# One written order of small steps for all five engines, and a first chunk in two halves of 256 tokens

## The chip, the cores and the metric

The kernel runs on one core of a Trainium2 chip. The metric is device microseconds of one execution; the kernel before takes 420.45 us (median of 3 runs, 420.3 to 420.76).

The engines are called by the names of the profile: PE (TensorE, its weight loads apart as PEld), DVE (VectorE), ACT (ScalarE), POOL (GpSimd) and SP (SyncE). POOL issues the loads from memory, SP the transposes by DMA and the stores of the output.

## What is computed

An attention of the linear kind over 8 batches of 8 heads, 576 tokens each, 64 wide, and behind it a two-layer block with an ELU over all 4608 tokens:

```python
def phi(x):
    proj = np.einsum('bhsd,df->bhsf', x, w_phi)                # 64 -> 128
    proj = proj - np.max(np.abs(proj), axis=-1, keepdims=True)
    return np.concatenate([np.exp(proj), np.exp(-proj)], axis=-1)
q_p, k_p = phi(q), phi(k)
kv = np.einsum('bhsf,bhsd->bhfd', k_p, v);  z = np.sum(k_p, axis=2)
num = np.einsum('bhsf,bhfd->bhsd', q_p, kv)
den = np.einsum('bhsf,bhf->bhs', q_p, z)[..., None] + 1e-06
x = (num / den) as 4608 x 512                                  # heads side by side
h = x @ w_in                                                   # 512 -> 2048
out = np.where(h > 0, h, np.exp(np.minimum(h, 0)) - 1) @ w_out # 2048 -> 512
```

## The kernel before

The attention goes by 16 groups n of four heads (two groups a batch). One group passes these stages; the name of a stage's product in PSUM is the one that the profile shows:

- `transpose_in`: k and q come with tokens on the partitions and are transposed to kT and qT. For the first four groups PE does it (tile `tr`) and DVE copies it out; for the others it is a DMA transpose on SP.
- `stage_k`, three pieces: PE projects (pk), DVE takes the largest absolute value of each row (mk), ACT writes both exponentials (EK). `scale_v`: ACT takes the exponentials of the row maxima (em), POOL multiplies v by them (vs, four large ones a group).
- `stage_qmax`, three pieces: PE projects q with tokens on the partitions (pm), DVE takes the row maxima (mq), splits them into a high and a low bf16 part (mhl), and they are transposed (mT).
- `stage_q`, three pieces: PE projects q with features on the partitions and subtracts the maxima by a product with the selector `sel` (pq); ACT writes both exponentials (Eq).
- `stage_kv`: 72 small products (kv), copied out by DVE (kv_sb).
- `stage_pn`, two pieces: 20 products (pn), of which DVE divides (den, rec, xp). `transpose_x` brings xp into xT_sb, for the first two groups by PE (trx) and DVE, then by two DMA transposes a piece.

The ELU block goes by 9 chunks of 512 tokens. Each has 16 first steps `moe_mm1` (four matmuls ph of 512 columns; ACT takes the exponential e_sb, POOL its minimum with 1, DVE the maximum with ph, into gT) and 16 second steps `moe_mm2` (four matmuls po; after every fourth step ACT copies o_sb and SP stores it). Chunk 0 needs only the tokens of batch 0, chunk c up to 7 those of batch c, and chunk 8 comes last.

The order is written as a list of pieces of one group, between which a number of `moe` steps is emitted from a list `pending`; a chunk joins that list some pieces after its batch is done (`LAG`). From this order and its own estimates a scheduler sets the order on each engine when the program is built. In PSUM the first 38 pieces use four tiles of two banks; after them there are two tiles of two banks (for pk, pm, pq, kv and pn) and four of one bank (for ph, po and the transposes).

The core's 16 DMA engines move the loads in the order in which POOL issues them. A load on POOL waits in the program until the load eight places before it has landed, since it takes over that one's semaphore.

Of the kernel before, what the change touches and what calls it, by code (L numbers as in the profile page):

```python
# [12 lines left out]
ALU = mybir.AluOpType  # L13
ACT = mybir.ActivationFunctionType


@with_exitstack
def kernel(
# [34 lines left out]
    PE_TRANSPOSED_X = 2  # L53
# [10 lines left out]
    pools = {}  # L64

    def two_banks(shape, dtype, name):
        return pools["pj"].tile(shape, dtype, name=name, tag="pj")

    def one_bank(shape, dtype, name):
        if "mp" in pools:  # L70
            return pools["mp"].tile(shape, dtype, name=name, tag="mp")
        return pools["pj"].tile(
            [shape[0], 2 * shape[1]] + shape[2:], dtype, name=name, tag="pj"
        )[:, 0:shape[1]]

    natural = {}

    def load(name, src, b, p0=0, p1=H // 2):
        if (name, b) not in natural:
            natural[name, b] = io.tile([P, H // 2, NS, D], BF16, name=name + "n")  # L80
        nc.gpsimd.dma_start(  # L81
            out=natural[name, b][:, p0:p1].rearrange("p r s d -> p r (s d)"),
            in_=src[b]
            .rearrange("h s d -> (h s d)")
            .rearrange("(pr q x) -> q pr x", q=P, x=NS * D)[:, p0:p1],
        )


    w_f32 = consts.tile([P, F], FP32)
    for par in range(2):  # L90
        nc.sync.dma_start(out=w_f32[par * D:(par + 1) * D, :], in_=w_phi)
    load("k", k, 0, 0, 2)
    ident = consts.tile([P, P], BF16)
    make_identity(nc, ident)
    load("k", k, 0, 2, 4)
    load("q", q, 0, 0, 2)
    load("v", v, 0, 0, 2)
    load("q", q, 0, 2, 4)
    load("v", v, 0, 2, 4)

    w_bd = consts.tile([P, 2, F], BF16)
    nc.vector.memset(w_bd, 0.0)
    for par in range(2):
        r = slice(par * D, (par + 1) * D)
        nc.vector.tensor_copy(w_bd[r, par, :], w_f32[r, :])

    sel_small = consts.tile([P, NI], BF16)
    nc.vector.memset(sel_small, 0.0)  # L110
    for off in (0, NI, D, D + NI):
        nc.gpsimd.affine_select(
            out=sel_small, in_=sel_small, pattern=[[-1, NI]],
            compare_op=ALU.not_equal, fill=-1.0, base=-off, channel_multiplier=1,
        )
    sel = consts.tile([P, NI, F], BF16)
    nc.vector.tensor_copy(sel, sel_small.unsqueeze(2).to_broadcast((P, NI, F)))

    load("k", k, 1)
    load("q", q, 1)  # L120
    w_in_sb = consts.tile([P, N_CT, DFF], BF16)
    w_in_r = moe_w_in.rearrange("(ct p) j -> p ct j", p=P)
    for c0 in range(0, N_CT, 2):
        nc.gpsimd.dma_start(out=w_in_sb[:, c0:c0 + 2, :], in_=w_in_r[:, c0:c0 + 2, :])
    load("v", v, 1)
    w_out_sb = consts.tile([P, N_JT, DM], BF16)
    w_out_r = moe_w_out.rearrange("(jt p) o -> p jt o", p=P)
    for jt in range(0, N_JT, 8):
        nc.gpsimd.dma_start(
            out=w_out_sb[:, jt:jt + 8, :], in_=w_out_r[:, jt:jt + 8, :]  # L130
        )

    mhl_bufs = []
    for j in range(2):
        mhl_j = consts.tile([P, 2, D], BF16, name=f"mhl{j}")
        nc.vector.memset(mhl_j, 0.0)
        mhl_bufs.append(mhl_j)

# [11 lines left out]
    def out_rows(tile_index):  # L150
        bp, t = divmod(tile_index, 9)
        rows = []
        for half in range(2):
            if t == 4:
                b, s = 2 * bp + half, 8
            else:
                b, t4 = (2 * bp, t) if t < 4 else (2 * bp + 1, t - 5)
                s = 4 * (t4 % 2) + t4 // 2 + 2 * half
# [5 lines left out]
    moe_state = {}  # L164

    def moe_mm1(ch, jt):
        t0 = ch * CHUNK
        if jt == 0:
            moe_state[ch] = moep.tile([P, N_JT, CHUNK], BF16, name="gT")
        gT = moe_state[ch]  # L170
        ph = one_bank([P, CHUNK], FP32, "ph")
        for ct in range(N_CT):
            nc.tensor.matmul(  # L173
                ph,
                w_in_sb[:, ct, jt * P:(jt + 1) * P],
                xT_sb[:, ct, t0:t0 + CHUNK],
                start=(ct == 0),
                stop=(ct == N_CT - 1),
            )
        e_sb = epool.tile([P, CHUNK], FP32, name="e_sb")  # L180
        nc.scalar.activation(e_sb, ph, ACT.Exp)  # L181
        nc.gpsimd.tensor_scalar(  # L182
            e_sb, e_sb, 1.0, 0.0, op0=ALU.min, op1=ALU.max
        )
        nc.vector.scalar_tensor_tensor(  # L185
            gT[:, jt, :], e_sb, -1.0, ph, op0=ALU.add, op1=ALU.max
        )

    def moe_mm2(ch, tt, part):
        gT = moe_state[ch]  # L190
        if part == 0:
            moe_state[ch, tt] = one_bank([P, DM], FP32, "po")
        po = moe_state[ch, tt]
        for jt in range(4 * part, 4 * part + 4):
            nc.tensor.matmul(  # L195
                po,
                gT[:, jt, tt * P:(tt + 1) * P],
                w_out_sb[:, jt, :],
                start=(jt == 0),
                stop=(jt == N_JT - 1),  # L200
            )
        if part == 3:
            o_sb = opool.tile([P, DM], FP32, name="o_sb")
            nc.scalar.copy(o_sb, po)  # L204
            for half, rows in enumerate(out_rows(ch * (CHUNK // P) + tt)):
                nc.sync.dma_start(out=rows, in_=o_sb[half * D:(half + 1) * D])

    pending = []

    def enqueue_chunk(ch):  # L210
        for jt in range(N_JT):
            pending.append((moe_mm1, ch, jt))
        for tt in range(CHUNK // P):
            for part in range(4):
                pending.append((moe_mm2, ch, tt, part))

    def emit_moe():
        if pending:
            fn, *args = pending.pop(0)
            fn(*args)  # L220

    st = {}
# [3 lines left out]
    SLOTS = (  # L226
        ((0, 0), (0, 2), (1, 0), (1, 2), (0, 3)),
        ((1, 4), (1, 6), (0, 5), (0, 7), (1, 7)),
    )

    def pe_transpose(dst, blocks):

        for j0 in range(0, len(blocks), 5):
            part = blocks[j0:j0 + 5]
            tr = one_bank([P, 8, P], BF16, "tr")
            for j, blk in enumerate(part):
                nc.tensor.transpose(tr[:, j, :], blk, ident)
            nc.vector.tensor_copy(dst[:, j0:j0 + len(part), :], tr[:, 0:len(part), :])

    def transpose_in(n, name):  # L240
        if n >= NG:
            return
        b, g = divmod(n, 2)
        nat = natural[name, b][:, 2 * g:2 * g + 2].rearrange("p r s d -> p (r s d)")
        dst = tpool.tile([P, NI, P], BF16, name=name + "T")
        if n < PE_TRANSPOSED:
            pe_transpose(dst, [nat[:, i * P:(i + 1) * P] for i in range(NI)])
        else:
            nc.sync.dma_start_transpose(out=dst, in_=nat)
        st[name + "T", n] = dst  # L250

    def row_max(m, pj, c):
        nc.vector.tensor_reduce(  # L253
            m[:, 6 * c:6 * c + 6], pj, axis=AX.X, op=ALU.max,
            apply_absolute_value=True,
        )

    def project_k(n, c):
        kT = st["kT", n]
        pj = two_banks([P, 8, F], FP32, "pk")  # L260
        for i3 in range(3):
            nc.tensor.matmul(  # L262
                pj[:, 2 * i3:2 * i3 + 2, :].rearrange("p r f -> p (r f)"),
                kT[:, 3 * c + i3, :],
# [4 lines left out]
        return pj[:, 0:6, :]  # L269

    def stage_k(n, c):
        if c == 0:
            st["EK", n] = work.tile([P, 2, 2 * NS, F], BF16, name="EK")
            st["mk", n] = small.tile([P, 2 * NS], FP32, name="mk")
            st["em", n] = small.tile([P, 2, 2 * NS], FP32, name="em")
            st["vs", n] = work.tile([P, 2, 2 * NS, D + 1], BF16, name="vs")
        EK, mk = st["EK", n], st["mk", n]
        pj = project_k(n, c)
        row_max(mk, pj, c)
        for sg in range(2):  # L280
            nc.scalar.activation(  # L281
                EK[:, sg, 6 * c:6 * c + 6, :], pj, ACT.Exp, scale=1.0 - 2.0 * sg
            )
        if c > 0:
            scale_v(n, c - 1)

    def scale_v(n, pr):
        b, g = divmod(n, 2)
        mk, em, vs = st["mk", n], st["em", n], st["vs", n]
        r = slice(pr * NS, (pr + 1) * NS)  # L290
        for sg in range(2):
            nc.scalar.activation(  # L292
                em[:, sg, r], mk[:, r], ACT.Exp, scale=2.0 * sg - 1.0
            )
        for sg in range(2):
            nc.gpsimd.tensor_tensor(  # L296
                vs[:, sg, r, 0:D],
                natural["v", b][:, 2 * g + pr],
                em[:, sg, r].unsqueeze(2).to_broadcast((P, NS, D)),
                op=ALU.mult,  # L300
            )
        nc.gpsimd.tensor_copy(vs[:, :, r, D], em[:, :, r])

    def stage_qmax(n, c):
# [18 lines left out]
        if c < 2:  # L323
            return
# [258 lines left out]
```

## Time and profile before

| | |
|---|---|
| runs | 420.45 us median (420.3 to 420.76) |
| profiled execution | 421.46 us, its span 419.7 us |
| busy | PE 370.2, DVE 247.8, ACT 246.8, POOL 189.7 us |
| mean clock granted to PE | 0.958 |
| first ph matmul | 43.29 us |
| moved by DMA | 40.08 MB, mean 95 GB/s |

The span runs from the first to the last instruction of the profiled execution. In lines of the profile a group of instructions has its source line, its engine and operation, what it writes and reads, how often it stands, its busy time and mean duration, and after the second bar the time that the engine stood idle before it and what ended most of that. Rows of the timeline begin with the start and the length in us, and end, in brackets, with the idle time before them and its cause.

### The profile page before, as it was taken

To read this page: it belongs to the slowest core of one execution; us is meant where nothing else is said; L and a number is where in the kernel's file an instruction comes from. 1 tells how busy PE (TensorE), PEld (TensorE's weight loads), DVE (VectorE), ACT (ScalarE), POOL (GpSimd) and SP (SyncE) were. 2 spreads that over 40 slices of the span, in tenths; PEclk is the share of its full clock that TensorE was granted. 3 is DMA by queue.
4 is the path that set the end of the run, shared out by engine and by line. 5 is a ranking of instruction groups with operands and counts; after the bars stand their busy time and mean duration, and the time that the engine had idled before them with its cause. 6 is when DMAs were issued, how large, how long until landed. Compare 5 with 4: busy or idle time off the path is not lost.

```text
span 419.7 us, 9524 instructions
## 1 busy us (share of the span) xinstructions
PE 370.2 (88%) x3856; PEld 194.0 (46%) x3856; DVE 247.8 (59%) x419; ACT 246.8 (59%) x437; POOL 189.7 (45%) x281
## 2 busy tenths in 40 slices
PE   3567787995989998999899989999799989999995
PEld 2356335452545454454445544545354535444442
DVE  4978566752776467645866477647754943360630
ACT  2747435753676667756774777487647772551631
POOL 8840651615265346534663366236604570450620
PEclk9659888998899999999999999999999999999999
DMA  8999972399128952879179813652143002203113
GB/s 120 210 211 208 194 105 44 64 169 183 33 58 131 157 104 45 112 117 176 30 114 146 161 27 58 135 110 36 30 89 74 19 16 66 66 2 75 25 27 75
DMA packets 69564, 40.08 MB, mean 95 GB/s; under 512 B 49936, under 2 KB 64400, under 8 KB 69520
## 3 DMA queue, kind: packets, MB, share of 16 engines
q0 software_dynamic: 15344, 18.35, 28.1%
q1 hardware_dynamic: 54176, 21.12, 27.3%
q8 instruction: 30, 0.49, 0.5%
q14 instruction: 14, 0.11, 0.1%
HBM read 36.77 MB, written 9.44 MB: 110 GB/s over the span
## 4 chain that ended last, share of the span: by engine, by line
PE 34%; DVE 22%; issue 18%; ACT 11%; POOL 10%; DMA 4%; POOLq 0%; ACTq 0%
PE po L195 17%; PE ph L173 10%; DVE gT L185 8%; POOL vs L296 5%; DVE mk L253 4%; POOL e_sb L182 4%; ACT EK L281 3%; DMA qT<-qn 3%; ACT Eq L370 3%; DVE xp L422 3%; ACT e_sb L181 3%; DVE mq L319 2%; PE pn L410 2%; PE kv L388 2%; PE pk L262 1%
## 5 line engine op out<-in xcount | busy, mean ns | idle before, releaser
L173 PE MATMUL ph<-xT_sb,w_in_sb 128*128 128x512 bf16 x576 | 143.0, 389 | 15.5 <-DVE gT L185 10.0
L185 DVE SCALAR_TENSOR_TENSOR gT<-e_sb,ph 128x512 bf16<-128x512 f32 x144 | 94.3, 684 | 75.7 <-POOL e_sb L182 75.5
L195 PE MATMUL po<-w_out_sb,gT 128*128 128x512 bf16 x576 | 137.6, 380 | 0.5 <-DVE gT L185 0.5
L182 POOL TENSOR_SCALAR e_sb<-e_sb 128x512 f32<-128x512 f32 x144 | 86.7, 613 | 110.9 <-ACT e_sb L181 110.7
L181 ACT ACTIVATE e_sb<-ph 128x512 f32<-128x512 f32 x144 | 83.4, 606 | 61.8 <-PE ph L173 61.6
L296 POOL TENSOR_TENSOR vs<-vn,em 128x576 bf16<-128x576 bf16 x64 | 72.4, 1152 | 59.4 <-ACT em L292 43.7
L173 PEld LDWEIGHTS <-w_in_sb 128*128 128x128 bf16 x576 | 54.4, 99 | 76.2 <-issue 16.5
L281 ACT ACTIVATE EK<-pk 128x768 bf16<-128x768 f32 x96 | 72.6, 814 | 23.4 <-DVE mk L253 21.5
L370 ACT ACTIVATE Eq<-pq 128x768 bf16<-128x768 f32 x96 | 73.5, 824 | 16.0 <-PE pq L360 15.7
L195 PEld LDWEIGHTS <-gT 128*128 128x128 bf16 x576 | 52.4, 98 | 55.6 <-DVE gT L185 1.0
L319 DVE TENSOR_REDUCE mq<-pm 128x6 f32<-128x768 f32 x48 | 45.9, 957 | 36.6 <-PE pm L312 36.5
L204 ACT COPY o_sb<-po 128x512 f32<-128x512 f32 x36 | 21.1, 587 | 67.0 <-PE po L195 42.9
L253 DVE TENSOR_REDUCE mk<-pk 128x6 f32<-128x768 f32 x48 | 45.5, 952 | 11.8 <-PE pk L262 11.8
L410 PEld LDWEIGHTS <-Eq 128*128 128x128 bf16 x640 | 24.0, 97 | 8.0 <-DVE kv_sb L396 0.6
L262 PE MATMUL pk<-w_bd,kT 128*128 128x256 bf16 x144 | 25.6, 293 | 1.9 <-ACT EK L281 0.8
L422 DVE TENSOR_TENSOR xp<-pn,rec 128x640 bf16<-128x640 f32 x32 | 26.4, 824 | 1.2 <-DVE rec L420 0.3
L410 PE MATMUL pn<-kv_sb,Eq 128*128 128x65 bf16 x640 | 25.4, 194 | 0.5 <-DVE kv_sb L396 0.4
L388 PEld LDWEIGHTS <-EK 64*128 64x128 bf16 x1152 | 20.9, 99 | 7.1 <-ACT Eq L370 3.5
L388 PE MATMUL kv<-vs,EK 64*128 64x65 bf16 x1152 | 22.9, 197 | 1.2 <-ACT Eq L370 1.1
L81 POOL DMA_DIRECT2D qn<-in_q_dram x9 | 6.8, 760 | 33.2 <-PE po L195 13.3
L312 PE MATMUL pm<-w_bd,qT 64*128 64x128 bf16 x288 | 18.2, 230 | 4.0 <-ACT EK L281 1.5
L262 PEld LDWEIGHTS <-kT 128*128 128x128 bf16 x144 | 14.1, 103 | 14.8 <-issue 5.2
(42 smaller groups left out, 164.8 us busy)
## 6 DMA issues: line engine op xcount, KB each, us to landing
out_dram<-o_sb SPq DMA_DIRECT2D x72, 128.0 KB, 2.5
kn<-in_k_dram POOLq DMA_DIRECT2D x7, 576.0 KB, 7.3
qn<-in_q_dram POOLq DMA_DIRECT2D x7, 576.0 KB, 7.7
vn<-in_v_dram POOLq DMA_DIRECT2D x7, 576.0 KB, 10.1
w_in_sb<-in_moe_w_in_dram POOLq DMA_DIRECT2D x2, 1024.0 KB, 19.0
w_out_sb<-in_moe_w_out_dram POOLq DMA_DIRECT2D x2, 1024.0 KB, 28.0
xT_sb<-xp SPq DMA_TRANSPOSE x56, 2.4
kn<-in_k_dram POOLq DMA_DIRECT2D x2, 288.0 KB, 5.5
```

What stands on the lines that cost most here:

```text
L173: nc.tensor.matmul(ph, w_in_sb[:, ct, jt * P:(jt + 1) * P], xT_sb[:, ct, t0:t0 + CHUNK], start=(ct == 0), stop=(ct == N_CT - 1),)
L181: nc.scalar.activation(e_sb, ph, ACT.Exp)
L182: nc.gpsimd.tensor_scalar(e_sb, e_sb, 1.0, 0.0, op0=ALU.min, op1=ALU.max)
L185: nc.vector.scalar_tensor_tensor(gT[:, jt, :], e_sb, -1.0, ph, op0=ALU.add, op1=ALU.max)
L195: nc.tensor.matmul(po, gT[:, jt, tt * P:(tt + 1) * P], w_out_sb[:, jt, :], start=(jt == 0), stop=(jt == N_JT - 1),)
L253: nc.vector.tensor_reduce(m[:, 6 * c:6 * c + 6], pj, axis=AX.X, op=ALU.max, apply_absolute_value=True,)
L281: nc.scalar.activation(EK[:, sg, 6 * c:6 * c + 6, :], pj, ACT.Exp, scale=1.0 - 2.0 * sg)
L296: nc.gpsimd.tensor_tensor(vs[:, sg, r, 0:D], natural["v", b][:, 2 * g + pr], em[:, sg, r].unsqueeze(2).to_broadcast((P, NS, D)), op=ALU.mult,)
L319: nc.vector.tensor_reduce(mq[:, 6 * c:6 * c + 6].rearrange("p (i r) -> p r i", r=2), pj[:, :, 0:3, :], axis=AX.X, op=ALU.max, apply_absolu ...
L370: nc.scalar.activation(Eq[:, sg, :, :, 3 * c * D:3 * (c + 1) * D].rearrange("p h r x -> p r h x"), pj[:, :, 0:3 * P].rearrange("p r (h x) ...
L388: nc.tensor.matmul(kv[:, hi, pr, sg, :], EK[rows, sg, pr * NS + s, :], vs[rows, sg, pr * NS + s, :], start=(s == 0), stop=(s == NS - 1),)
L410: nc.tensor.matmul(pn[:, hi, t, :], Eq[:, sg, hi, par, i0 * D:(i0 + 2) * D], kv_sb[:, hi, pr, sg, :], start=(sg == 0), stop=(sg == 1),)
```

## The change

The stages are cut into steps of one engine each (43 kinds, such as `k_mm`, `k_exp`, `k_max`), a string names 1709 steps by one letter each, and the program is written in exactly that order: `manual_schedule` leaves the order on each engine as written. The order was worked out elsewhere by list scheduling. A part of it:

```diff
+ORDER = """
+eabecedjfkfAjgBhkBAhCeBjfABkjiBCliBlkAmDgmlCBFlemBAmDfCBFBMNECEMNDAOEPBQMENBFCSEDUETTFEMVOENPWQM
...
+    pjp = ctx.enter_context(tc.tile_pool(name="pjp", bufs=2, space=bass.MemoryType.PSUM))
+    mpp = ctx.enter_context(tc.tile_pool(name="mpp", bufs=4, space=bass.MemoryType.PSUM))
+
+    ctx.enter_context(tc.manual_schedule(engines=None))
...
+    FIRST = 2
+    PIECES = (((0, 4), (4, 7), (7, 9)), ((0, 3), (3, 6), (6, 9)))
...
+    def m_split(n, part):
+        if n < FIRST:
+            p = ((0, 4), (4, NI))[part]
+        else:
+            p = (0, NI)
+        hi = mhl[n % 2][:, :, p[0]:p[1]]
+        mq = st["mq", n][:, :, p[0]:p[1]]
+        eng = nc.gpsimd if n < PE_TRANSPOSED else nc.vector
+        eng.tensor_copy(hi, mq)
+        eng.tensor_tensor(
+            mhl[n % 2][:, :, NI + p[0]:NI + p[1]], mq, hi, op=ALU.subtract
+        )
...
+    def x_parts(n, part):
+        if n < FIRST:
+            return [(pr, t) for pr in range(2) for t in ((0, 1), (2, 3, 4))[part]]
+        return [(part, t) for t in range(5)]
...
+    chunk_parts = [
+        (ch, jt, h, h + w)
+        for ch in range(N_CHUNK)
+        for w in [CHUNK // 2 if ch == 0 else CHUNK]
+        for h in range(0, CHUNK, w)
+        for jt in range(N_JT)
+    ]
...
+        M=(m_mm, groups(*THIRDS, first=HALVES)), N=(m_max, groups(*THIRDS, first=HALVES)),
+        O=(m_split, m_parts),
...
+        p=(h_mm, chunk_parts), q=(h_exp, chunk_parts), r=(h_min, chunk_parts),
+        s=(h_elu, chunk_parts),
+        t=(o_mm, [(*x, part) for x in o_tiles for part in range(4)]),
+        u=(o_copy, o_tiles), v=(o_store, o_tiles),
     )
...
+    queues = {letter: (fn, iter(args)) for letter, (fn, args) in STEPS.items()}
+    for letter in "".join(ORDER.split()):
+        fn, args = queues[letter]
+        fn(*next(args))
```

For groups 0 and 1 the tokens are placed so that the first 256 of chunk 0 need only the first piece of four (of nine) of pm and pq and the first part of pn: chunk 0 is computed in two halves, with 32 first steps of 256 columns instead of 16 of 512, and its second half needs the other pieces. For those groups q is cut 4, 3, 2 instead of 3, 3, 3, mhl is split in two parts, and xT gets each part for two heads' columns at once. For the first four groups mhl is written by POOL instead of DVE. The two large and four small PSUM tiles now serve from the start. The loads come in smaller parts for k of batch 0, v of batch 0 in one, and w_in ahead of k and q of batch 1.

On POOL, in the head of the program, this is how the last loads and the first products stand before (vn and w_out_sb are loads like w_in_sb; vs is v times em):

```order
L124 DMA w_in_sb<-in_moe_w_in_dram 128x2x2048
L112 AFFINE_SELECT sel_small<-sel_small 128x9
L124 DMA w_in_sb<-in_moe_w_in_dram 128x2x2048
L81 DMA vn<-in_v_dram 128x4x576
L129 DMA w_out_sb<-in_moe_w_out_dram 128x8x512 x2
L296 TENSOR_TENSOR vs<-vn,em 128x9x64 x2
L302 CAST vs<-em 128x2x9
```

(the loads of k and q of batch 1 stand just ahead of these, and those of batch 2 follow after all vs of groups 0 and 1), and this is how they stand now:

```order
L194 DMA w_in_sb<-in_moe_w_in_dram 128x2x2048 x2
L185 DMA kn<-in_k_dram 128x4x576
L185 DMA qn<-in_q_dram 128x4x576
L198 DMA w_out_sb<-in_moe_w_out_dram 128x8x512 x2
L185 DMA vn<-in_v_dram 128x4x576
L275 CAST vs<-em 128x2x9
L185 DMA kn<-in_k_dram 128x4x576
L185 DMA qn<-in_q_dram 128x4x576
L275 CAST vs<-em 128x2x9
L266 TENSOR_TENSOR vs<-vn,em 128x9x64 x2
L310 CAST mhl_96<-mq 128x2x4
L311 TENSOR_TENSOR mhl_96<-mq,mhl_96 128x2x4
```

What moved: w_in stands ahead of the loads of batch 1, the loads of k and q of batch 2 stand ahead of the first vs, and group 0's mhl stands behind two vs. The second qn load here takes over the semaphore of w_in's first half.

On DVE, where the maxima of group 0 are made ready and what follows from them, before (mq and mk are row maxima of q and k, mT the transposed maxima, kv_sb a copy):

```order
L319 TENSOR_REDUCE mq<-pm 128x2x3
L238 COPY qT<-tr 128x640
L327 CAST mhl_131<-mq 128x2x9
L238 COPY qT<-tr 128x512
L328 TENSOR_TENSOR mhl_131<-mq,mhl_131 128x2x9
L238 COPY mT<-tr 128x128
L319 TENSOR_REDUCE mq<-pm 128x2x3 x3
L327 CAST mhl_133<-mq 128x2x9
L328 TENSOR_TENSOR mhl_133<-mq,mhl_133 128x2x9
L396 CAST kv_sb<-kv 128x520
```

and now:

```order
L297 TENSOR_REDUCE mq<-pm 128x2x4
L322 COPY mT<-tr 128x128
L297 TENSOR_REDUCE mq<-pm 128x2x3
L248 TENSOR_REDUCE mk<-pk 128x6
L409 CAST kv_sb<-kv 128x520
L297 TENSOR_REDUCE mq<-pm 128x2x2
L322 COPY mT<-tr 128x128
L443 TENSOR_SCALAR den<-pn 128x2x4
L444 RECIPROCAL rec<-den 128x2x4
L446 TENSOR_TENSOR xp<-pn,rec 128x2x4x64
```

The mhl rows are gone from DVE, the first mT is copied after four of nine pieces of each group's q, and the first xp, of 8 instead of 10 parts, comes before the rest of the maxima.

More of the change, by code (lines that the diff above doesn't have):

```diff
@@ L76 @@
[L76 to L91, printed above, removed]
@@ L92 @@
-    load("k", k, 0, 0, 2)
-    ident = consts.tile([P, P], BF16)
[L94 to L99, printed above, removed]
+        return mpp.tile(shape, dtype, name=name, tag="mp")
+    ident = consts.tile([P, P], BF16)
     w_bd = consts.tile([P, 2, F], BF16)
[L102 to L105, printed above, removed]
@@ L122 @@
     w_in_r = moe_w_in.rearrange("(ct p) j -> p ct j", p=P)
-    for c0 in range(0, N_CT, 2):
-        nc.gpsimd.dma_start(out=w_in_sb[:, c0:c0 + 2, :], in_=w_in_r[:, c0:c0 + 2, :])
-    load("v", v, 1)
     w_out_sb = consts.tile([P, N_JT, DM], BF16)
     w_out_r = moe_w_out.rearrange("(jt p) o -> p jt o", p=P)
[L128 to L137, printed above, removed]
+    mhl = [consts.tile([P, 2, D], BF16, name=f"mhl{j}") for j in range(2)]
@@ L189, in moe_mm2 @@
[L189 to L206, printed above, removed]
@@ L240, in transpose_in @@
[L240 to L255, printed above, removed]
-        )
@@ new lines, in start, with weights @@
+    def start():
+        w_f32 = epool.tile([P, CHUNK], FP32, name="e_sb")[:, 0:F]
+        for par in range(2):
+            nc.sync.dma_start(out=w_f32[par * D:(par + 1) * D, :], in_=w_phi)
+        st["w_f32"] = w_f32
+        make_identity(nc, ident)
+    def weights():
+        nc.vector.memset(w_bd, 0.0)
+        nc.vector.memset(sel_small, 0.0)
+        for j in range(2):
+            nc.vector.memset(mhl[j], 0.0)
+        for par in range(2):
+            r = slice(par * D, (par + 1) * D)
+            nc.vector.tensor_copy(w_bd[r, par, :], st["w_f32"][r, :])
@@ L357, in stage_q, with places @@
-        for i3 in range(3):
+            r = []
+            for j in range(w):
+                i = PLACE_OF[own][par][p0 + j]
+                if r and i == PLACE_OF[own][par][p0 + j - 1] + 1:
+                    r[-1][2] += 1
+                else:
+                    r.append([j, i, 1])
+            runs.append(r)
+        def places(par, j, m):
+            return pj[:, par, 0:w * P].rearrange("p (h i t) -> p h i t", h=2, i=w)[
+                :, :, j:j + m, :
+            ]
+        for x in range(max(len(r) for r in runs)):
+            for par in range(2):
+                if x >= len(runs[par]):
+                    continue
+                j, i, m = runs[par][x]
+                rows = slice(par * D, (par + 1) * D)
+                nc.tensor.matmul(
+                    places(par, j, m),
+                    w_bd[rows, par, :],
+                    qT[rows, i:i + m, :].rearrange("p i (h t) -> p h i t", h=2),
+                    start=(x == 0),
+                    stop=False,
+                )
@@ L358, in stage_q @@
+        for j in range(w):
             for par in range(2):
@@ L550, with h_mm @@
-    after_piece()
-    while pending:
-        emit_moe()
+                out=xT_sb[:, ct, mixed_col(b):mixed_col(b) + D].unsqueeze(1),
+                in_=xp[D:P, 4].rearrange("p h d -> p (h d)"),
+            )
+    def h_mm(ch, jt, h0, h1):
+        ph = one_bank([P, CHUNK], FP32, "ph")[:, h0:h1]
+        for ct in range(N_CT):
+            nc.tensor.matmul(
+                ph,
+                w_in_sb[:, ct, jt * P:(jt + 1) * P],
+                xT_sb[:, ct, ch * CHUNK + h0:ch * CHUNK + h1],
+                start=(ct == 0),
+                stop=(ct == N_CT - 1),
+            )
+        st["ph", ch, jt, h0] = ph
@@ new lines, in o_mm, with o_copy @@
+    def o_mm(ch, tt, part):
+        po = get(("po", ch, tt), lambda: one_bank([P, DM], FP32, "po"))
+        for jt in range(4 * part, 4 * part + 4):
+            nc.tensor.matmul(
+                po,
+                st["gT", ch][:, jt, tt * P:(tt + 1) * P],
+                w_out_sb[:, jt, :],
+                start=(jt == 0),
+                stop=(jt == N_JT - 1),
+            )
+    def o_copy(ch, tt):
+        st["o", ch, tt] = opool.tile([P, DM], FP32, name="o_sb")
+        nc.scalar.copy(st["o", ch, tt], st["po", ch, tt])
@@ new lines, in o_store, with groups @@
+    def o_store(ch, tt):
+        for half, rows in enumerate(out_rows(ch * (CHUNK // P) + tt)):
+            nc.sync.dma_start(out=rows, in_=st["o", ch, tt][half * D:(half + 1) * D])
+    def groups(*tails, first=None):
+        if first is None:
+            return [(n, *x) for n in range(NG) for x in tails]
+        head = [(n, *x) for part in first for n in range(FIRST) for x in part]
+        return head + [(n, *x) for n in range(FIRST, NG) for x in tails]
+    PAIR = [(0,), (1,)]
+    THIRDS = [(c,) for c in range(3)]
@@ new lines, with blocks @@
+    THIRDS2 = [(c, sg) for c in range(3) for sg in range(2)]
+    HALVES = ([(0,)], [(1,), (2,)])
+    HALVES2 = (THIRDS2[:2], THIRDS2[2:])
+    EACH = ([(0,)], [(1,)])
+    PT = PE_TRANSPOSED
+    def blocks(name, n):
+        cut = 3 if (name, n) == ("k", 0) else 5
+        return [(name, n, 0, cut), (name, n, cut, NI)]
+    m_parts = groups((0,), first=EACH)
+    chunk_parts = [
[4 more added lines that the diff above has]
+        for jt in range(N_JT)
+    ]
@@ L556 @@
+    queues = {letter: (fn, iter(args)) for letter, (fn, args) in STEPS.items()}
+    for letter in "".join(ORDER.split()):
+        fn, args = queues[letter]
+        fn(*next(args))
+    assert all(next(args, None) is None for _, args in queues.values())
 _INS = ['q', 'k', 'v', 'w_phi', 'moe_w_in', 'moe_w_out']
```

504 lines of the change are left out of this document (240 added, 264 removed).

## The prediction

> **What bounds the kernel now.** I read the page first, then the busy time by stretches, then TensorE's (PE's) instructions in order of time.
>
> ```profile
> span 419.7 us, 9524 instructions
> PE 370.2 (88%) x3856; PEld 194.0 (46%) x3856; DVE 247.8 (59%) x419; ACT 246.8 (59%) x437; POOL 189.7 (45%) x281
> GB/s 120 210 211 208 194 105 44 64 169 183 33 58 131 157 104 45 112 117 176 30 114 146 161 27 58 135 110 36 30 89 74 19 16 66 66 2 75 25 27 75
> ```
> PE is the fullest engine, and 49.5 us of its span are idle. The next fence cuts the span where the first matmul of chunk 0 (43.29), the first of chunk 1 that had all its tokens (103.88) and the attention-free end (359.83) stand; 119.5 to 334.6 is five whole batches.
>
> ```profile
> 0.00:43.29 43.29, 24.21 (x414) 17.77 (x415) 31.67 (x61) 22.77 (x39) 24.50 (x40) 0.80 1.09 188
> 43.29:103.88 60.59, 49.80 (x511) 25.62 (x507) 34.78 (x59) 32.51 (x58) 26.60 (x38) 0.89 0.82 122
> 103.88:359.83 255.95, 240.95 (x2681) 125.71 (x2682) 159.30 (x267) 167.17 (x299) 119.00 (x172) 0.99 0.49 86
> 119.50:334.60 215.10, 201.92 (x2272) 105.87 (x2271) 137.96 (x231) 144.91 (x261) 104.65 (x151) 1.00 0.55 93
> 359.83:419.70 59.87, 55.25 (x256) 24.85 (x254) 22.00 (x32) 24.37 (x41) 19.59 (x32) 0.99 0.19 45
> ```
> The columns after the length are PE, PEld, DVE, ACT, POOL, clock, DMA share, GB/s. The last stretch is full but for its 4.6 us drain; the first three are not.
>
> Busy time flatters PE, since matmuls overlap in it. So I price PE's work by the distance between starts:
>
> ```profile
> 206.72 1.03 PE L173 MATMUL ph<-xT_sb,w_in_sb 128*128 128x512 bf16 x4
> 209.32 1.02 PE L173 MATMUL ph<-xT_sb,w_in_sb 128*128 128x512 bf16 x4 [1.57 <-DVE gT L185]
> ...
> 218.57 1.32 PE L388 MATMUL kv<-vs,EK 64*128 64x65 bf16 x72
> 219.82 0.82 PE L195 MATMUL po<-w_out_sb,gT 128*128 128x512 bf16 x3
> ...
> 221.90 0.79 PE L410 MATMUL pn<-kv_sb,Eq 128*128 128x65 bf16 x20
> 222.53 1.89 PE L195 MATMUL po<-w_out_sb,gT 128*128 128x512 bf16 x8
> 224.26 0.49 PE L262 MATMUL pk<-w_bd,kT 128*128 128x256 bf16 x3
> 224.58 1.89 PE L195 MATMUL po<-w_out_sb,gT 128*128 128x512 bf16 x8
> ...
> 235.84 0.34 PE L350 MATMUL pq<-qT,w_bd 64*128 64x384 bf16 x2
> 236.01 0.33 PE L360 MATMUL pq<-mT,sel 64*128 64x128 bf16 x6
> 236.18 0.33 PE L312 MATMUL pm<-w_bd,qT 64*128 64x128 bf16 x6
> 236.44 1.47 PE L173 MATMUL ph<-xT_sb,w_in_sb 128*128 128x512 bf16 x6
> ...
> 373.48 13.98 PE L195 MATMUL po<-w_out_sb,gT 128*128 128x512 bf16 x64
> 387.29 13.98 PE L173 MATMUL ph<-xT_sb,w_in_sb 128*128 128x512 bf16 x64
> ```
> 64 wide matmuls take 387.29 - 373.48 = 13.81 us, a step of four 0.863, a chunk 27.6. A head group takes kv 1.25, two pn 1.26, three pk 0.96, three times pq 0.34 and pm 0.26: 5.3 us. One chunk and two groups are 38.2 us, and a batch takes 215.1/5 = 43.0: PE loses 4.8 us a batch. 1.7 of it is the gap at 207.6, where the next four ph wait for a PSUM bank that VectorE's gT frees; the rest are pauses of 0.1 to 0.5.
>
> **The change, term by term.** Nothing on PE gets cheaper, so what can be won is PE's lost time, and I sum four stretches.
>
> *To the first ph.* The new order puts the loads of w_in ahead of k and q of batch 1, moves two more loads (k and q of batch 2) ahead of group 0's vs on POOL, moves the mhl pair of the first four groups from DVE to POOL behind those vs, and gives the head two large PSUM tiles where it had four. The rows:
>
> ```profile
> kn<-in_k_dram POOLq DMA_DIRECT2D x7, 576.0 KB, 7.3
> DMA to landing us min/median/max: 17.1/19.0/20.9
> 8.20 0.74 POOL L124 DMA_DIRECT2D w_in_sb<-in_moe_w_in_dram  x1
> 10.70 0.76 POOL L81 DMA_DIRECT2D vn<-in_v_dram  x1 [0.75 <-DMA qn<-in_q_dram]
> 19.86 3.92 DVE L327 CAST mhl<-mq 128x18 bf16<-128x18 f32 x1
> 106.56 1.51 ACT L370 ACTIVATE Eq<-pq 128x768 bf16<-128x768 f32 x2 [1.38 <-PE pq L360]
> ...
> L181 ACT ACTIVATE e_sb<-ph 128x512 f32<-128x512 f32 x144 | 83.4, 606 | 61.8 <-PE ph L173 61.6
> L370 ACT ACTIVATE Eq<-pq 128x768 bf16<-128x768 f32 x96 | 73.5, 824 | 16.0 <-PE pq L360 15.7
> L296 POOL TENSOR_TENSOR vs<-vn,em 128x576 bf16<-128x576 bf16 x64 | 72.4, 1152 | 59.4 <-ACT em L292 43.7
> L319 DVE TENSOR_REDUCE mq<-pm 128x6 f32<-128x768 f32 x48 | 45.9, 957 | 36.6 <-PE pm L312 36.5
> L422 DVE TENSOR_TENSOR xp<-pn,rec 128x640 bf16<-128x640 f32 x32 | 26.4, 824 | 1.2 <-DVE rec L420 0.3
> L396 DVE CAST kv_sb<-kv 128x520 bf16<-128x520 f32 x16 | 11.1, 695 | 4.2 <-PE kv L388 4.2
> L302 POOL CAST vs<-em 128x18 bf16<-128x18 f32 x32 | 8.3, 259 | 0.0
> L238 DVE COPY kT<-tr 128x640 bf16<-128x640 bf16 x4 | 1.9, 485 | 1.9 <-PE tr L237 1.9
> ```
> The row at 10.70 shows the wait: POOL stood until an older load (qn) had landed. The new q load of batch 2 waits in the same way for the load eight places back, which is now w_in's first half. That half landed at 8.20 + 17.1 = 25.3 us; without k and q of batch 1 ahead of it (2 x 0.59 MB at 211 GB/s, 5.6 us) it lands at 19.7. Behind the wait stand all vs of groups 0 and 1. POOL then does the load (0.78), a cast (0.26), two vs (2.3) and the mhl pair, which it never did: at least DVE's 0.2, at most the 3.92 that the cast took on DVE; nearest is POOL's cast of the same 18 elements, 2 x 0.26. That gives 23.5.
> From there, with only two large tiles, each product waits for the tile before last: copy 0.2, mq 0.9, mk 0.9 and latencies (25.8); pq 0.9 at the low clock, two Eq a third wider 2.2 (28.9); kv copy 0.7, mq 0.6 (30.2); pn 0.8, xp chain 1.1 (32.1); copy 0.2, mq 0.9, xT copy 0.4, mq 0.6 (34.2); kv 1.3, copy 0.7 (36.2); pn 0.8, xp 1.1 (38.1); three copies 1.1, xT copy 0.4 (39.6). First ph at **40 us**, against 43.29. Ends: 34, where POOL isn't held and vs start as now; 46, where w_in lands no earlier than now.
> Rule against row: the Trainium skill's "SBUF — State Buffer" (section "SBUF: two separate sides") says that VectorE and GpSimd share a port pair as an exclusive lock, and who loses blocks. The 3.92 us row lies beside vs and agrees. By that rule alone the move to POOL would bring 3.7 us and the first ph would come at 36; I don't take it, since the pair now queues behind those vs.
>
> *Chunk 0, to the first ph of chunk 1.* PE: 16 ph steps and 16 po steps, 27.6 us, and by the order 2.8 groups, 14.8: 42.4. A 256-wide matmul costs half (pk's three take 0.32, 0.107 each), so the halves cost PE nothing, and their loads hide as pk's do. ACT: 33 wide exponentials (two in 1.51, so 0.76 each) 25, four copies and six small pairs 4, 32 half-wide ones between 0.30 and 0.61, taken 0.40: 12.8, in all 42. So ACT is as full as PE, and 16 more instructions on it lie on the path (3 us, in the sum). With both full I take 1.2 times the work: **51 us**; ends 42.4 and 60.6 (as now). Chunk 1 starts at 91, against 103.88.
>
> *To the end of the attention.* 256 us now, in a dense order 256 x 38.2/43.0 = 227. Chunk steps and attention steps alternate more finely now, with po between the ph, which attacks the 1.7 us gap; the 0.1 us pauses at each change to a 64-row product stay. I halve the loss: **241 us**; ends 227 and 256. Where a gT no longer holds the ph, ACT is late next (145 of 215 us busy).
>
> *End.* The same 256 matmuls and drain: **59.9 us** (here each wait has its cover: nothing but ELU work is left).
>
> 40 + 51 + 241 + 59.9 = 391.9 us of span. The profiled execution took 421.46 us for its span of 419.7; the median, 420.45, lies 0.75 above that span, so 392.7. Any change under 0.2% (0.8 us) couldn't be told from none.
>
> **Rivals.**
> *The middle stays as it is* (other pauses replace the gT gap: ACT is busy 145/5 = 29 us of each batch, mostly where a chunk's ph run, and feeds both kinds of step): 91 + 256 + 59.9 + 0.75 = 408.
> *Dense*: POOL isn't held and PE waits little: 36 + 46 + 233 + 59.9 + 0.75 = 376. Against it: in chunk 0 ACT is as full as PE.
> *Slower: late transposes.* One place now shows the price:
>
> ```profile
> 98.26 0.60 PE L173 MATMUL ph<-xT_sb,w_in_sb 128*128 128x512 bf16 x2
> 103.88 1.89 PE L173 MATMUL ph<-xT_sb,w_in_sb 128*128 128x512 bf16 x4 [5.01 <-DMA xT_sb<-xp]
> ```
> The ph waited 5.0 us for xT and then ran four matmuls in 1.89 instead of 1.03. In the new order only two or three po steps (1.7 to 2.6 us) and a small product or two lie between the last xT transpose of a batch and the first ph of its chunk, at chunks 1, 2, 4, 5, 6 and 7, and PE can't pass a waiting ph. 5.0 + 0.9 at all six is 35 us: 428. It decides from 4.6 us each. Against it: only there did loads fill the DMA engines; over the five batches their share is 0.55.
> By the Trainium skill, "TensorE: Matmul & The Clock Gate" (section "Part 1: The HAM clock gate"), an idle window of some 3.4 us halves PE's clock for a next one; the slow four agree, and by that rule each such wait would cost about 6.7 us, six of them 433.
> *No change*: every term at its upper end, 46 + 60.6 + 256 + 59.9 = 422.
>
> **How the numbers follow.** Forecast (384 to 401) 0.52, middle unchanged 0.21, dense 0.15, slower 0.09, no change 0.03. Leaving out what lies under 376 and over 409 leaves about 2 in 10 outside. Faster 0.52 + 0.21 + 0.15 = 0.88, same 0.03, slower 0.09.
>
> **What would show it.** POOL's row for q of batch 2 waiting for w_in until about 20 us, vs only after it, and the first 256-wide ph near 40 us; wrong if vs start by 15. First ph of chunk 1 near 91, with PE and ACT both about 0.8 busy before it. Between there and the tail, wide steps 0.86 apart and no gap over 1 us but at chunk starts; a wait on xT of over 2 us there would speak for the slower rival, and 43 us a batch for the unchanged middle. The forecast fails most likely in the size of the chunk 0 stretch, where no row of now shows ACT and PE both full.

## The result and the profile after

The changed kernel takes 397.9 us (median of 4 runs, 393.38 to 400.01) against 420.38 for the kernel before on the same chip: a ratio of 0.943 [0.935, 0.952]. The forecast was 392.7, with a range of 376 to 409. Run again it gave 395.4 us, 0.945 [0.940, 0.950]. A ratio is taken from the means of the fast executions alone; here it leaves out the slowest of the four, 1.7% above the fastest.

The profiled execution is that slowest one, 400.01 us. Three lines of its page, and then its stretches, cut at the first ph (42.36), the first ph of chunk 1 (93.80) and the start of the last 256 matmuls (338.40), as before; the columns are those of the prediction.

```profile
span 398.2 us, 9735 instructions
PE 364.5 (92%) x3928; PEld 199.4 (50%) x3928; DVE 244.0 (61%) x427; ACT 248.7 (62%) x453; POOL 194.1 (49%) x309
PE 74%; DMA 10%; POOL 6%; DVE 5%; issue 2%; ACT 2%; SPq 0%; POOLq 0%; ACTq 0%
```

```profile
0.00:42.36 42.36, 22.89 (x353) 17.59 (x354) 22.73 (x46) 17.49 (x29) 25.30 (x47) 0.76 1.07 181
42.36:93.80 51.44, 47.28 (x632) 31.18 (x630) 38.36 (x82) 37.51 (x82) 27.86 (x55) 1.00 0.88 129
93.80:338.40 244.60, 239.10 (x2696) 125.75 (x2693) 161.28 (x269) 170.54 (x305) 122.12 (x178) 0.99 0.59 95
338.40:398.20 59.80, 55.22 (x256) 24.85 (x254) 21.62 (x32) 23.21 (x39) 18.86 (x31) 0.99 0.17 40
```

The third line is the chain of work that ended last: TensorE (PE) holds 74% of it. Against the stretches of before (43.29, 60.59, 255.95, 59.87) the time was won in chunk 0, 9.15 us, and in the middle, 11.35; the head gave 0.9 and the end nothing. In the middle PE idles 244.60 - 239.10 = 5.5 us, before it was 15.0.

What PE still waits for is in its three longest rows of waits (us in all, times, longest), and in two places of GpSimd's (POOL's) and PE's timelines. The second row is the start of the loads, which took 5.7 us before:

```profile
PE tr L317 <- POOL mhl L311: 6.9, 2, 5.9
PE tr L207 <- DMA kn<-in_k_dram: 4.8, 1, 4.8
PE ph L500 <- DMA xT_sb<-xp: 4.3, 3, 2.4
```

```profile
21.06 0.74 POOL L185 DMA_DIRECT2D qn<-in_q_dram  x1 [4.12 <-DMA w_in_sb<-in_moe_w_in_dram]
21.80 0.28 POOL L275 CAST vs<-em 128x18 bf16<-128x18 f32 x1
21.96 2.27 POOL L266 TENSOR_TENSOR vs<-vn,em 128x576 bf16<-128x576 bf16 x2
24.17 0.18 POOL L310 CAST mhl<-mq 128x8 bf16<-128x8 f32 x1
24.43 0.21 POOL L311 TENSOR_TENSOR mhl<-mq,mhl 128x8 bf16<-128x8 f32 x1
...
118.98 1.92 POOL L516 TENSOR_SCALAR e_sb<-e_sb 128x512 f32<-128x512 f32 x3
128.70 0.79 POOL L185 DMA_DIRECT2D qn<-in_q_dram  x1 [7.80 <-DMA qT<-qn]
```

```profile
24.70 0.29 PE L317 MATMUL tr<-ident,mhl 128*128 128x128 bf16 x1 [5.87 <-POOL mhl L311]
...
133.36 0.38 PE L500 MATMUL ph<-xT_sb,w_in_sb 128*128 128x512 bf16 x1 [1.05 <-DMA xT_sb<-xp]
136.13 2.29 PE L500 MATMUL ph<-xT_sb,w_in_sb 128*128 128x512 bf16 x5 [2.40 <-DMA xT_sb<-xp]
```

In the head POOL stands 4.12 us at the load of q of batch 2 until w_in has landed; vs and mhl follow, and PE waits 5.87 us for mhl. At chunk 2 the transposes into xT are 3.45 us late (1.05 + 2.40). POOL's standing for 7.80 us from 120.9 holds nothing up: the last three minima of chunk 1 are done before it, and the vs behind it waits for ACT's em in any case. The row comes back below.

The gap that the forecast set out from, ph waiting for gT, is gone; the first row is of before:

```profile
PE ph L173 <- DVE gT L185: 10.0, 8, 1.6
PE ph L500 <- DVE gT L520: 0.2, 1, 0.2
```

### The profile page after: what moved, and what is told of

The parts are those of the page before. It is cut to its first block, busy times and chain, and to the rows that moved or that the text cites. A ratio compares the mean times of both kernels' runs of the same rounds, so it can differ in the third digit from the quotient of the medians.

```text
span 398.2 us, 9735 instructions
## 1 busy us (share of the span) xinstructions
PE 364.5 (92%) x3928; PEld 199.4 (50%) x3928; DVE 244.0 (61%) x427; ACT 248.7 (62%) x453; POOL 194.1 (49%) x309
## 4 chain that ended last, share of the span: by engine, by line
PE 74%; DMA 10%; POOL 6%; DVE 5%; issue 2%; ACT 2%; SPq 0%; POOLq 0%; ACTq 0%
PE po L528 28%; PE ph L500 28%; PE pn L429 4%; PE kv L398 4%; DMA w_in_sb<-in_moe_w_in_dram 3%; DMA xT_sb<-xp 3%; PE pk L230 3%; POOL vs L266 3%; PE pq L359 2%; DMA kT<-kn 2%; PE pm L285 2%; PE pq L369 2%; DVE xp L446 1%; DVE gT L520 1%; DVE mq L297 1%
## 5 line engine op out<-in xcount | busy, mean ns | idle before, releaser
L500 PE MATMUL ph<-xT_sb,w_in_sb 128*128 128x512 bf16 (+1 forms) x640 | 140.2, 362 | 4.9 <-DMA xT_sb<-xp 4.3
L516 POOL TENSOR_SCALAR e_sb<-e_sb 128x512 f32<-128x512 f32 (+1 forms) x160 | 90.4, 573 | 106.7 <-ACT e_sb L511 105.9
L520 DVE SCALAR_TENSOR_TENSOR gT<-e_sb,ph 128x512 bf16<-128x512 f32 (+1 forms) x160 | 97.2, 629 | 47.2 <-POOL e_sb L516 46.4
L511 ACT ACTIVATE e_sb<-ph 128x512 f32<-128x512 f32 (+1 forms) x160 | 86.5, 567 | 39.7 <-PE ph L500 36.6
L500 PEld LDWEIGHTS <-w_in_sb 128*128 128x128 bf16 x640 | 59.3, 98 | 62.1 <-issue 6.5
L381 ACT ACTIVATE Eq<-pq 128x768 bf16<-128x768 f32 (+2 forms) x96 | 72.4, 819 | 15.2 <-PE pq L369 14.8
L297 DVE TENSOR_REDUCE mq<-pm 128x6 f32<-128x768 f32 (+2 forms) x48 | 45.4, 953 | 24.5 <-PE pm L285 24.4
L248 DVE TENSOR_REDUCE mk<-pk 128x6 f32<-128x768 f32 x48 | 45.3, 953 | 19.7 <-ACT EK L241 11.2
L446 DVE TENSOR_TENSOR xp<-pn,rec 128x640 bf16<-128x640 f32 (+2 forms) x32 | 26.4, 824 | 1.1
L285 PE MATMUL pm<-w_bd,qT 64*128 64x128 bf16 x288 | 16.2, 224 | 3.5 <-DVE mq L297 2.0
L257 ACT ACTIVATE em<-mk 128x9 f32<-128x9 f32 x64 | 10.1, 219 | 14.5 <-DVE mk L248 14.4
```

The lines of the kernel that those rows point to most:

```text
L297: nc.vector.tensor_reduce(mq[:, :, p0:p1], st["pm", n, c][:, :, 0:p1 - p0, :], axis=AX.X, op=ALU.max, apply_absolute_value=True,)
L381: nc.scalar.activation(Eq[:, sg, :, :, p0 * D:p1 * D].rearrange("p h r x -> p r h x"), st["pq", n, c][:, :, 0:(p1 - p0) * P].rearrange("p ...
L500: nc.tensor.matmul(ph, w_in_sb[:, ct, jt * P:(jt + 1) * P], xT_sb[:, ct, ch * CHUNK + h0:ch * CHUNK + h1], start=(ct == 0), stop=(ct == N_ ...
L511: nc.scalar.activation(e_sb, st["ph", ch, jt, h0], ACT.Exp)
L516: nc.gpsimd.tensor_scalar(e_sb, e_sb, 1.0, 0.0, op0=ALU.min, op1=ALU.max)
L520: nc.vector.scalar_tensor_tensor(gT[:, jt, h0:h1], st["e", ch, jt, h0], -1.0, st["ph", ch, jt, h0], op0=ALU.add, op1=ALU.max,)
```

## The experiments

**The same kernel again**, to know its scatter.

> The changed kernel once more, unchanged, to see how far its times scatter. If the scatter of 393.4 to 400.0 us comes from transposes that land before or after PE needs them, this profile has another set of waits of ph on xT than the first (4.3 us in three waits) and its span differs by about as much, with the first ph again at 42 us +-0.5. If it comes from something else (a lower clock all through), the waits on xT stay at 4.3 us and the wide matmuls' spacing differs from 0.216.

Measured: 395.39 us (394.04 to 399.35), 0.9448 [0.9401, 0.9495]; the profiled execution, its fastest, has a span of 392.3, first ph at 41.81, chunk 1 at 93.28. Its row of waits for xT is shorter:

```profile
PE ph L500 <- DMA xT_sb<-xp: 1.6, 1, 1.6
```

Head and chunk 0 repeat to 0.6 us, the rest took 299.0 us instead of 304.4. So the profile above is 5.4 us worse behind chunk 0 than this one; 2.7 of it are waits for xT, and the rest I did not part. (Right behind its wait of 2.40 us five matmuls take 2.29 us, and the granted clock from 130 to 140 us is 0.73, in the repeat 1.00.)

**The load of q of batch 2 behind the vs of group 1**, nothing else. (In a diff like this one each line is a letter of the order, with the step that it stands for.)

```diff
 D  v_exp    group 0, half 1
-f  load     q of batch 2
 C  k_max    group 1, piece 0
...
 E  v_scale  group 1, half 1, sign 1
+f  load     q of batch 2
```

> Only the load of q of batch 2 moves on POOL, from ahead of the first vs to behind the last vs of group 1. If the wait of that load for w_in's landing sets the head (the forecast's step), vs start 6 us earlier (near 15 us), PE's wait for mhl falls from 5.9 us to under 1, the first ph comes at 37 us instead of 42.4 and the time falls by 4 to 5 us, to about 393. Rival: the two large PSUM tiles and DVE's own work set the head, and then vs start earlier but the first ph moves by less than 2 us and the time stays at 396 to 398.

Measured: 391.66 us, 0.9341 [0.9297, 0.9384]; first ph at 36.67. Its POOL, and its PE:

```profile
15.88 0.74 POOL L185 DMA_DIRECT2D kn<-in_k_dram  x1 [2.13 <-DMA vn<-in_v_dram]
16.61 0.27 POOL L275 CAST vs<-em 128x18 bf16<-128x18 f32 x1
16.77 2.26 POOL L266 TENSOR_TENSOR vs<-vn,em 128x576 bf16<-128x576 bf16 x2
```

```profile
19.50 0.29 PE L317 MATMUL tr<-ident,mhl 128*128 128x128 bf16 x1 [0.60 <-POOL mhl L311]
```

The two vs start 5.2 us earlier than at 21.96, and the first ph comes 5.1 to 5.7 us earlier. PE's wait for mhl falls from 5.87 to 0.60 us. The time follows by 3.7 us. That the load holds the head is shown.

**mhl on VectorE (DVE) for all groups**, as before the change.

```diff
-        eng = nc.gpsimd if n < PE_TRANSPOSED else nc.vector
+        eng = nc.vector
```

> The changed kernel with the two small instructions that split mq into mhl on VectorE for all groups, as in the kernel before, instead of on GpSimd for groups 0 to 3. Theory (in the head the pair queues on GpSimd behind the v scalings, which a load holds until 21 us; without the pair there kv of group 0 still needs those scalings, which end at about 27 us): TensorE's wait of 5.6 to 5.9 us for mhl goes, kv of group 0 starts at 26.5 to 27 us instead of 27.3, the later waits for mhl of 0.7 to 1.0 us go too, and the first ph comes at 39.5 to 41.3 us instead of 41.8 to 42.4; time 393 to 395. Rival (VectorE is the fuller engine there, or is held up by GpSimd's work on the same tiles, the shared port of the Trainium skill's SBUF page): first ph at 42 to 44 us, 395 to 398.

Measured: 397.68 us, 0.9439 [0.9391, 0.9488], not to be told from the changed kernel; first ph at 43.41, so the rival's number. DVE's rows, then POOL's at the same time:

```profile
19.29 0.16 DVE L310 CAST mhl<-mq 128x8 bf16<-128x8 f32 x1
...
26.87 0.70 DVE L409 CAST kv_sb<-kv 128x520 bf16<-128x520 f32 x1 [4.57 <-PE kv L398]
27.48 3.37 DVE L310 CAST mhl<-mq 128x8 bf16<-128x8 f32 x1
30.88 0.17 DVE L311 TENSOR_TENSOR mhl<-mq,mhl 128x8 bf16<-128x8 f32 x1
```

```profile
26.20 2.25 POOL L266 TENSOR_TENSOR vs<-vn,em 128x576 bf16<-128x576 bf16 x2
28.41 0.25 POOL L275 CAST vs<-em 128x18 bf16<-128x18 f32 x1
28.56 2.26 POOL L266 TENSOR_TENSOR vs<-vn,em 128x576 bf16<-128x576 bf16 x2
```

Group 0's mhl came at once (19.29), as the theory had it. But the cast of eight columns for group 1, 0.16 us elsewhere, took 3.37 and ended at 30.85, when POOL's last vs ended (30.82). The copy of kv from PSUM at 26.87, beside the same vs, took its normal 0.70. The Trainium skill, "SBUF — State Buffer" (section "SBUF: two separate sides"), has this as a port pair that the later of the two engines waits for. These rows agree, but for one thing: the Trainium skill's page has the pair taken for one instruction, and here the cast waited until a whole row of POOL's instructions had ended. The move of mhl to POOL so brought 1.0 to 1.6 us of head, not the 3.7 that the rule alone would have given.

**No order held**: the same steps in the same sequence, but the scheduler orders each engine, as in the kernel before.

```diff
-    ctx.enter_context(tc.manual_schedule(engines=None))
```

> The same steps written in the same sequence, but the engines' order is again set by the scheduler that the kernel before used, with its own estimates. If the exact order on each engine is what pays (the forecast), the middle falls back towards 256 us and chunk 0 towards 60, and the time is 405 to 420. If cutting the work into steps, the halves of chunk 0 and the sequence pay, and the scheduler keeps close to the sequence, the time is within 2 us of the changed kernel's 398.

Measured: 426.72 us, 1.0145 [1.0094, 1.0196], 1.5% over the kernel before and outside both expectations. Its stretches up to the last 256 matmuls (first ph 41.83, chunk 1 98.86):

```profile
0.00:41.83 41.83, 24.90 (x352) 17.74 (x353) 23.00 (x46) 17.75 (x29) 24.89 (x47) 1.00 1.08 184
41.83:98.86 57.03, 48.19 (x625) 32.19 (x630) 38.50 (x82) 37.49 (x82) 28.49 (x56) 0.97 0.74 122
98.86:367.00 268.14, 241.61 (x2657) 128.17 (x2693) 160.80 (x269) 171.26 (x305) 121.05 (x177) 0.97 0.50 86
```

The head is the same. Chunk 0 loses 5.6 us and the middle 23.5, and 21.0 of these are idle time of PE (26.5 against 5.5). PE's waits of ph for gT are back, too:

```profile
PE ph L499 <- DVE gT L519: 6.0, 8, 2.2
```

So the finer steps, in the order that the scheduler gives them, win nothing.

**The order alone**: the kernel before, its coarse stages held to the order in which they are written.

```diff
+    ctx.enter_context(tc.manual_schedule(engines=None))
```

> The kernel before, each engine held to the order in which its program is written (the scheduler takes no part). If what was lost before was lost to the scheduler's reordering, this gains: the 1.7 us gap of each batch goes and the time is 405 to 415. If the coarse pieces themselves are at fault (each piece written through, so that an engine waits for the others inside a piece), it is slower than before: 430 us or more.

Measured: 508.71 us, 1.2117 [1.2076, 1.2158]. The coarse stages in their held order cost 89 us, the fine steps without a held order 7. Coarse stages in an order worked out for being held were not tried, so that the gain needs the fine steps is not shown.

**Which engine's order it is.** Four kernels with the changed kernel's steps hold only some engines:

```diff
-    ctx.enter_context(tc.manual_schedule(engines=None))
+    ctx.enter_context(tc.manual_schedule(engines={nc.tensor.engine}))
```

and likewise with the other four, with DVE and POOL, and with ScalarE (ACT).

> All steps of the changed kernel, but only TensorE is held to the written order; VectorE, ScalarE, GpSimd and SyncE get theirs from the scheduler, as in the kernel before. With all five held it took 395.4 us, with none 426.7. Theory (the gain of the fixed order is that TensorE always has dense work to fill with; the others follow it): 396 to 403. Rival (what counts is that exps, minima and elu steps come in the order in which TensorE needs them): 412 to 427, with the lost time as waits of TensorE on gT, kv_sb and Eq in the middle stretch, which took 244.6 us in the changed kernel and 268.1 with no order held.

> The other half: VectorE, ScalarE, GpSimd and SyncE are held to the written order, TensorE's order is left to the scheduler. Theory (TensorE's order carries the gain): 412 to 427. Rival (the order of the four that feed it carries it): 395 to 403. If both halves are needed, this and the run with TensorE alone are both above 405.

> Only VectorE and GpSimd are held to the written order; TensorE, ScalarE and SyncE are left to the scheduler. All four but TensorE held: 396.2 us; TensorE alone: 430.6; none: 426.7. Theory (what costs time is VectorE standing at an elu step until GpSimd's minimum is there, 85 us in all with no order held against 46 with all held, with copies of kv and maxima that TensorE needs queued behind it): 395 to 402. Rival (ScalarE's order of exps carries it): 412 to 430 here and 395 to 402 with ScalarE alone.

> Only ScalarE is held to the written order. Theory (VectorE and GpSimd carry it): 412 to 430. Rival (ScalarE's order of exps carries it, and the engines behind it follow): 395 to 402.

| held | time, us | ratio to before | DVE's gT waits for POOL's e_sb, us |
|---|---|---|---|
| all five, again | 395.39 | 0.9448 [0.9401, 0.9495] | 43.1 |
| all but PE | 396.19 | 0.9445 [0.9409, 0.9481] | 44.5 |
| DVE and POOL | 397.62 | 0.9468 [0.9418, 0.9518] | 43.7 |
| ACT | 427.87 | 1.0184 [1.0130, 1.0238] | 80.9 |
| PE | 430.64 | 1.0263 [1.0219, 1.0307] | 86.6 |
| none | 426.72 | 1.0145 [1.0094, 1.0196] | 85.0 |

My theory for the first two, that holding PE's order carries the gain, fell: PE alone gives none of it, and without PE held nothing is lost. DVE's and POOL's orders together are enough; neither was held alone. How far the scheduler goes from the written order can be counted in the traces, by kind of instruction. On PE 3643 of 3928 weight loads stand in their written place with no order held, and 3614 with DVE and POOL held; so PE's order hardly differs in any of the six, and what quite another one would cost was not tried. On DVE 280 of 427 instructions and on POOL 217 of 318 stand in place with no order held, and none is more than 7 places off.

What happens between them is seen with no order held, at PE's longest wait of the middle; POOL, DVE and PE in turn:

```profile
131.23 0.61 POOL L515 TENSOR_SCALAR e_sb<-e_sb 128x512 f32<-128x512 f32 x1 [1.64 <-ACT e_sb L510]
136.31 0.79 POOL L184 DMA_DIRECT2D qn<-in_q_dram  x1 [4.46 <-DMA qT<-qn]
137.13 0.62 POOL L515 TENSOR_SCALAR e_sb<-e_sb 128x512 f32<-128x512 f32 x1
```

```profile
137.79 0.69 DVE L519 SCALAR_TENSOR_TENSOR gT<-e_sb,ph 128x512 bf16<-128x512 f32 x1 [5.22 <-POOL e_sb L515]
138.39 0.69 DVE L408 CAST kv_sb<-kv 128x520 bf16<-128x520 f32 x1
```

```profile
138.53 0.61 PE L527 MATMUL po<-w_out_sb,gT 128*128 128x512 bf16 x1 [4.69 <-DVE gT L519]
```

POOL has a load of q in its order ahead of a chunk's last minimum. The load waits until its buffer is read out, the minimum stands behind it, DVE stands at the elu step with kv's copy behind, and PE waits 4.69 us for that step's gT. The next longest wait of the middle, 4.18 us at 224, has the same rows: a load of q on POOL at 225.00, then the minima, the elu steps, kv's copy. In the changed kernel this load of q waits still longer, the 7.80 us above, but all minima of the chunk stand ahead of it. These two places are 8.9 of the 21.0 us; the other waits are between 0.2 and 2.1 us, and I did not trace each. No run moved these two loads alone, so their cost is read from the rows and not shown by an experiment.

**Chunk 0 in one piece.** The steps of its first half are left out, those of the second take 512 columns, and the output products of its first two token tiles move behind them (p, q, r, s: ph, exponential, minimum, elu).

```diff
-        for w in [CHUNK // 2 if ch == 0 else CHUNK]
+        for w in [CHUNK]
```

> The changed kernel with chunk 0 in one piece of 512 tokens, as in the kernel before: the 16 steps of each kind for the first half are left out, those of the second half take the whole width, and the output products of the first two token tiles move behind them into the start of chunk 1; all else keeps its order. Theory (the half chunk gives TensorE dense work of 16 times 0.52 us, 8.3 us, between 41.8 and 61 us, where it would otherwise wait): the first ph comes at about 54 to 62 us, TensorE idles 5 to 8 us more before chunk 1, 400 to 404 us. Rival (the halves cost as much as they fill, since half as wide instructions have the same fixed cost on ScalarE, GpSimd and VectorE): 393 to 397.

Measured: 405.46 us, 0.9694 [0.9653, 0.9734], 10.1 us more than the changed kernel's repeat, above what the theory gave. First ph at 62.20. The stretch in which the first half would have run, here and then in the repeat of the changed kernel:

```profile
41.80:62.20 20.40, 12.47 (x150) 8.32 (x151) 14.03 (x24) 11.41 (x21) 6.55 (x11) 0.64 1.07 174
```

```profile
41.80:62.20 20.40, 17.78 (x226) 12.68 (x225) 18.42 (x39) 16.04 (x35) 12.07 (x26) 1.00 1.04 175
```

PE is busy 5.3 us less, and its work there runs at a granted clock of 0.64 instead of 1.00, which my count left out. At the first ph of chunk 1 this profile is 4.2 us behind the repeat (97.44 against 93.28) and has done 40 po matmuls where the repeat had done 64, 24 fewer, which the prediction's spacing (0.863 for four) puts at 5.2 us. So an estimated 9.4 of the 10.1 us are lost by then, and the moved output products cost little but their own length, which falls due later. The two halves carry about 10 of the change's 25 us.

**Three loads later.** The loads of k of batch 5, v of batch 4 and q of batch 5 move behind chunk 2's first two ph steps.

```diff
-e  load     k of batch 5
...
-g  load     v of batch 4
...
-f  load     q of batch 5
...
 p  h_mm     chunk 2, step 1
...
+e  load     k of batch 5
+g  load     v of batch 4
+f  load     q of batch 5
```

> The changed kernel with the loads of k of batch 5, v of batch 4 and q of batch 5 moved on GpSimd from ahead of the transposes of batch 2 into xT to behind chunk 2's first two ph steps. Theory (these transposes are late at chunk 2 because the three loads are in flight beside them): TensorE's wait for xT at chunk 2, 1.6 us in the repeat, 2.3 with q of batch 2 moved and 3.5 in the first profile, is under 0.3 us, and the time is 1.5 to 4 us under the changed kernel's 395.4: 391.5 to 394. Rival (the transposes are late because x_div in front of them is): the wait stays at 1.6 to 3.5 us and the time at 394 to 397. Second rival: the loads are late now, and batch 4's v scaling or batch 5's transposes wait for them: a new wait of 1 us or more later in the middle, 395 to 400.

Measured: 394.10 us, 0.9392 [0.9360, 0.9424]. PE's waits from chunk 1 to the end are now

```profile
PE ph L500 <- DVE gT L520: 0.4, 2, 0.2
PE pk L230 <- DVE xp L446: 0.2, 1, 0.2
```

with no wait for xT left. The four transposes for chunk 2 took a median of 8.0 us from issue to landing in the first profile, and 2.4 here: the loads beside them made them late. The median time is 1.3 us lower than the repeat's; the intervals of the two ratios overlap, so that this gain in time isn't shown.

**Both moves of loads together**, the version that the runs pointed to.

> Both mends together: the load of q of batch 2 behind the last v scaling of group 1 (alone 391.7 us), and the three loads of batches 4 and 5 behind chunk 2's first two ph steps (alone 394.1 against 395.4). Theory (the two waits lie in different places and both on TensorE's path): first ph at 36 to 37 us, no wait for xT at chunk 2, 388.5 to 391. Rival (a transposition that is early here makes another late, or the clock takes the gain back): 391 to 394, with a wait for xT of over 1 us at another chunk's start.

Measured: 388.33 us (386.05 to 390.06), 0.9275 [0.9234, 0.9316], 7 us under the changed kernel's repeat and just under the theory's range. First ph at 37.26, no wait for xT. What the place of w_in ahead of batch 1's loads and the PSUM tiles of the head give was not tried by itself.

## Why the prediction was right, step by step

- *To the first ph, 40*: measured 42.36, again 41.81. The mechanism was right: the q load waits for w_in (until 21.06; "w_in lands at 19.7" was 1.4 early), then load, cast, two vs and the mhl pair on POOL at 0.2 each, mhl done at 24.64 (23.5). The chain from there took 17.7 us, forecast 16.5. Moving that one load took the wait away, and the first ph came 5 us earlier.
- *Chunk 0, 51*: measured 51.44. Right in size, half right in reason. The half-wide exponentials take 0.400 us, as taken, but ACT is busy 37.5 of 51.4 us (0.73) where I had 42 and it as full as PE: the durations of its rows there add up to 41.2, but neighbours overlap. PE is busy 0.92 in the profile; my 0.8 was by distances between starts, and 42.4 of 51.4 is still that. The factor 1.2 held, but no row stood behind it, so that is luck in part; "ACT as full as PE" did not hold.
- *The middle, 241*: measured 244.6, and 5.4 us less for everything behind chunk 0 when run again. Right in size, wrong in cause. I laid the gain to a finer alternation on PE. With no order held PE has nearly the same alternation, and the stretch takes 268; so it is not enough, and whether it is needed stays open. What the gain hangs on is the order of DVE and POOL, where minima and elu steps no longer stand behind a load or a wait. The gap that I quoted, ph waiting for gT, was a sign of that: 10.0 us in all before, 6.0 with no order held, 0.2 in the changed kernel. Half of the loss was a guess between two ends, so that the size came out is luck in part.
- *End, 59.9*: 59.80.
- *Middle unchanged* (408) didn't come; with no order held the stretch is longer still, 268 us. *Slower, late transposes*: its mechanism came at chunk 2, 3.45 us in the first profile, and hardly at chunk 1 (0.89), instead of 5 us at all six; at chunk 2 the loads were beside it, as the price's own row had them. *Dense* (376): its head came when the load was moved, but its 233 for the middle did not (237.4 in the best version, from the first ph of chunk 1 at 91.02, PE busy 233.28).
- By the rule on the clock gate in the Trainium skill ("TensorE: Matmul & The Clock Gate", section "Part 1: The HAM clock gate"), an idle window costs clock as well. The 0.64 in the experiment on chunk 0 agrees in part: the clock fell beside idle time, but no single gap there was over 1.8 us. Nor does each wait cost clock: behind the wait of 2.40 us above, five matmuls took 2.29 us, and behind one of 2.30 with q of batch 2 moved they took 1.24.

## What to carry to other kernels

Where engines run in order, look for the instruction that waits for something far away (a load waiting for its buffer or for an older load) and ask what stands behind it: here PE waited 4 to 6 us a time behind such loads on POOL in different versions, and placing one of them behind the work that others need was worth 3.7 us. The fullest engine's order need not be the one that is wrong: here a third of the places on the two engines that feed PE, off by 7 at most, made some 29 us. Hold one engine at a time to find out, and count how far each order really moved. A right total doesn't show a right cause: the middle came within 4 us for a reason that the runs didn't bear out.

## What the runs showed of the hardware that I had not expected

A small cast on VectorE from SBUF to SBUF waited not for one GpSimd instruction but for a row of them: 3.37 us over what was left of the two vs, a cast and two more vs that ran back to back, while a copy from PSUM beside them went on. And a PE that is busy in bursts, 61% over 20 us, was granted 0.64 of its clock there, with no gap over 1.8 us. So short gaps can cost more than their length: 5.3 us less busy there went with some 9.4 us lost by the start of chunk 1, as estimated above.
